# Attention's products in plain float32 on row halves and quarters of TensorE, without split operands

## The chip, the cores and the metric

The kernel runs on one core of a Trainium2 chip. The metric is the device time of one execution in microseconds (us), the median of several runs. Engines: PE is TensorE's products, PEld its weight loads, DVE is VectorE, ACT is ScalarE, POOL is GpSimd, SP is SyncE, which issues most transfers.

## The reference

Attention with a mix over the 12 heads before and after the softmax, then two MLPs, all in float32. B, H, S, D are 4, 12, 448, 64; 1792 tokens, model width 768, hidden width 2048.

```python
scores = scale * np.matmul(q, k.transpose(0, 1, 3, 2))
scores = np.einsum('bhij,hg->bgij', scores, w_pre)
scores = scores - np.max(scores, axis=-1, keepdims=True)
attn = np.exp(scores)
attn = attn / (np.sum(attn, axis=-1, keepdims=True) + 1e-09)
attn = np.einsum('bhij,hg->bgij', attn, w_post)
attn_out = np.matmul(attn, v)
...
h = x @ w_in;  r = np.maximum(h, 0.0);  x = (s * (r * r) + b) @ w_out
...
h = x @ w_in;  out = (h * np.cos(h)) @ w_out
```

## The kernel before

The rows of queries of a batch are cut into 4 blocks of 110 or 120 rows (BLOCKS); 16 blocks in all. For a block, the scores of each head (rows on partitions, 448 keys along) are copied from PSUM to SBUF and moved by DMA into a tile m with 120 partitions, 10 query rows times 12 heads, so that a product with a block-diagonal 120x120 matrix mixes the heads of 10 rows at once. Such a group of 10 rows is a tile of the loop; there are 180. m has two places, one block each.

Values that need more than one pass of fp32r are split into a high and a low part. Names and lines of the profile:
- queries (tq L389, qh and ql L394, L396) and keys (tk L320 for the first batch, L350 for the others; ks L327 to L363) are transposed by TensorE and split; queries are loaded twice and transposed once a block.
- scores (sps L420): two fp32r products a head, copies s on ACT or DVE (L431, L433), a transfer into m on SP's queue.
- The first mix: mh (L500 on ACT, L502 on POOL) is the high part of m, POOL subtracts it in place (L505), then three fp32r products (p L510 to L512).
- maximum (st L521, DVE), exp with its sum (e L528, ACT), small steps (L535, L537), and the weights w of the second mix, w_post by the reciprocals (L541, DVE).
- The second mix: plain float32, e as the stationary operand, four products of 120 columns a tile (a L550), copied to at (L562 ACT, L564 DVE).
- products with the values (vps L587): plain float32, two outputs of 64 partitions each beside one another, which is a column half of the array; copies xo (L599, L601) and transfers to x in DRAM.
- mlp (L620 on) then runs both MLPs from fp32r parts; its weights are prepared on ACT, DVE and POOL while it runs.

The order on every engine is written ahead by a planner (Plan): each step has a position, engines with costs, the steps that it follows, and holds on rings of buffers ("ps", "pa", "pp" are PSUM banks for scores and transposes, second mix, first mix: 4, 2 and 2). The planner runs through time and lets an engine take the waiting step with the lowest position whose buffers are free. The chip then executes each engine's instructions in that order. Positions come from STEP and LEAD and from offsets (OFF, W1 to W3, PRO, VW, AVP, AVL).

Of the kernel before, what the change touches and what calls it, by code (L numbers as in the profile page):

```python
# [20 lines left out]
R = 10  # L21
# [163 lines left out]
def constants():  # L185
    c = np.zeros((128, 128 + R), np.float32)
    c[:, :128] = np.eye(128)
    for r in range(R):
        c[r * 12:(r + 1) * 12, 128 + r] = 1.0
    return c  # L190


STEP = 2364.9
LEAD = 17549.5


def attention(pl, tc, q, k, v, w_pre, w_post, cst, x, mid, left, right, psl, psr):
# [4 lines left out]
    L = R * H  # L202
# [3 lines left out]
    st_p = pool(left, "a_st", 4)  # L206
# [3 lines left out]
    h_p = pool(left, "a_h", 2)  # L210
# [3 lines left out]
    q_p = pool(right, "a_q", 2, side="right")  # L214
    rk_p = pool(right, "a_rk", 2, side="right")
    rq_p = pool(right, "a_rq", 2, side="right")
# [4 lines left out]
    for name, cap in (("at", 2), ("e", N_E), ("h", 2), ("xo", 2), ("w2", 2), ("st", 4), ("m", 2), ("q", 2), ("rk", 2), ("rq", 2),   # L221
                      ("s", N_S), ("ps", 4), ("pa", 2), ("pp", 2), ("v0", 1), ("v1", 1), ("v2", 1), ("v3", 1)) + tuple((f"k{g}", 1) for g in range(6)):
# [7 lines left out]

    tiles, first = [], []
    parts = lambda n: ((0, 40), (40, 80)) if n == 0 else ((0, BLOCKS[n % 4][1]),)
    part_of = lambda n, t: sum(t * R >= r0 for r0, _ in parts(n)) - 1
    for n in range(NBLK):
        b, (i0, rows) = n // 4, BLOCKS[n % 4]
        first.append(len(tiles))
        tiles += [dict(n=n, b=b, t=t) for t in range(rows // R)]
# [21 lines left out]
    mask = one.tile([L, R], F32, name="mask")  # L259
    w12 = one.tile([L, 2, H], F32, name="w12")  # L260
    wp_h = one.tile([L, L], F32R, name="wp_h")
    wp_l = one.tile([L, L], F32R, name="wp_l")
    wq = one.tile([L, H, R], F32, name="wq")
    d_id = dma(-5200, lambda: ident, lambda: cst[:, 0:128], 65536, cost=450.0)
    d_mk = dma(CST, lambda: mask, lambda: cst[0:L, 128:128 + R], 4800)
    d_w = [dma(CST, lambda i=i: w12[:, i], lambda w=w: w.rearrange("(o h) g -> o h g", o=1).to_broadcast([R, H, H]), 5760, cost=950.0) for i, w in enumerate((w_pre, w_post))]
    hw = pl.hold("e")
    wide = lambda a: a.rearrange("p (r o) -> p r o", o=1).to_broadcast([L, R, H])

    def blk():  # L270
        hw.tile = e_p.tile([L, S], F32, tag="e", name="wblk")
        nc.vector.tensor_tensor(out=hw.tile[:, :L].rearrange("p (r h) -> p r h", h=H), in0=w12[:, 0:1].to_broadcast([L, R, H]), in1=wide(mask), op=ALU.mult)
    c0 = pl.add(LEAD - 11000, "dve", 200, blk, d_w + [d_mk], take=[hw])
    c1 = pl.add(LEAD - 11000, "act", 200, lambda: nc.scalar.activation(out=wp_h, in_=hw.tile[:, :L], func=AF.Copy, scale=D ** -0.5), [c0])
    c2 = pl.add(LEAD - 11000, "dve", 200, lambda: nc.vector.scalar_tensor_tensor(out=wp_l, in0=hw.tile[:, :L], scalar=D ** -0.5, in1=wp_h.bitcast(F32), op0=ALU.mult, op1=ALU.subtract), [c1], use=[hw])
    c3 = pl.add(LEAD - 11000, "dve", 200, lambda: nc.vector.tensor_tensor(
        out=wq, in0=w12[:, 1].rearrange("p (g o) -> p g o", o=1).to_broadcast([L, H, R]),
        in1=mask.rearrange("p (o r) -> p o r", o=1).to_broadcast([L, H, R]), op=ALU.mult), d_w + [d_mk])

    kh, k_done = {}, {}

    KW = 8 * D
    mh, m_first, m_done, m_sub, later, s_last = {}, {}, {}, {}, [], []
    m_all = m_p.tile([128, 2, 12 * S], F32R, name="m")

# [3 lines left out]
    piece = lambda z, i, n: at_all[:, z].rearrange("p c h w -> p (c h w)")[:, i:i + n]  # L291

    def first_keys(g, p):

        hk = kh[0, g] = pl.hold(f"k{g}")
        hr = scratch[0]
        raw = lambda: piece(0, 3 * g * KW, KW)[:CH].rearrange("p (x d) -> p x d", d=D)
        both = lambda: piece(0, (3 * g + 1) * KW, 2 * KW)[:CH].rearrange("p (x a d) -> p x a d", a=2, d=D)
        d = []
        for h in range(2):  # L300
            d.append(dma(p - 6000, lambda h=h: raw()[:, 4 * h:4 * h + 4].rearrange("p z d -> p (z d)"), lambda h=h: k[0, 2 * g + h].rearrange("(p z) d -> p (z d)", z=4),
                         CH * KW * 2, behind=d[-1:] + [s_open], two=g < 2, cost=500.0, rate=300.0))

        def hi(e):
            o = both()[:, :, 0].bitcast(F32R)
            if e == "pool":
                nc.gpsimd.tensor_scalar(out=o, in0=raw(), scalar1=1.0, scalar2=0.0, op0=ALU.mult, op1=ALU.add)
            else:
                nc.scalar.activation(out=o, in_=raw(), func=AF.Copy)
# [3 lines left out]
        for h in range(2):  # L313
# [3 lines left out]
            def trans(h=h, hp=hp, bank=bank, tag=tag):  # L317
                hp.tile = bank.tile([128, 512], F32, tag=tag, name="tk")[:, :S]
                for z in range(4):
                    nc.tensor.transpose(hp.tile[:, z * CH:(z + 1) * CH], both()[:, 4 * h + z].rearrange("p a d -> p (a d)"), ident[:CH, :CH])  # L320
# [88 lines left out]
    def scores(n, g, p):  # L409
        b, (i0, rows) = n // 4, BLOCKS[n % 4]  # L410
        if g == 0:
            mh[n] = pl.hold("m")
# [600 lines left out]
```

## Time and profile before

| | |
|---|---|
| time, 3 runs | median 1431.83 us (1430.13 to 1432.35) |
| profiled execution | span 1425.0 us from the first to the last instruction; its own time isn't listed, the median of the runs is 6.8 us above the span |
| TensorE products / weight loads | 1396.4 us (98%) / 1217.1 us (85%) |
| VectorE, ScalarE, POOL | 1189.2 (83%), 751.4 (53%), 635.4 us (45%) |
| transfers | 128.85 MB, mean 90 GB/s |

Busy times are sums of records and overlap where an engine works on several instructions; the mean duration of a TensorE record is longer than its share of the array's time, which shows in the chain of waits and in the distance between starts. A plain float32 product has two records, each with its weight load; an fp32r product and a transpose have one. "fp32r" products appear as f32 in the rows.

### The profile page before, as it was taken

The page shows a single profiled execution, that of the slowest core. Times are in us where ns is not written, and L with a number is a line of the kernel's source. Part 1 is how long each engine was busy: PE and PEld are TensorE (multiplying, and loading weights), DVE is VectorE, ACT ScalarE, POOL GpSimd, SP SyncE. Part 2 cuts the span into 40 slices and gives each one's busy share as a digit, 9 for nine tenths or more (in the row PEclk, how much of TensorE's full clock was granted, in tenths as well). Part 3 has the DMA queues.
Part 4 walks back from the last instruction along what each step waited for, and adds up shares of the span by engine and source line. Part 5 has one row for each costly group of instructions (what it writes and reads, how often), then busy time and mean ns, then how long its engine had stood idle before and what let it go on. Part 6 is the DMA issues. An engine that isn't in the chain of part 4 may idle for free.

```text
span 1425.0 us, 23242 instructions
## 1 busy us (share of the span) xinstructions
PE 1396.4 (98%) x8268; PEld 1217.1 (85%) x8269; DVE 1189.2 (83%) x2195; ACT 751.4 (53%) x1587; POOL 635.4 (45%) x579
## 2 busy tenths in 40 slices
PE   8999999999999899999999999999999999999999
PEld 6788888888887678888888888889999999999998
DVE  6888788688787888988887877888799999999975
ACT  4668677677677565332333232356645545455442
POOL 3746455564465354333333242334554454544431
PEclk9999999999999999999999999999999999999999
DMA  5755656565464432221211211111111121211103
GB/s 160 185 143 147 152 134 159 129 153 144 119 154 140 127 125 70 72 59 56 68 56 56 67 45 45 56 34 56 56 56 45 56 59 53 67 45 56 56 34 122
DMA packets 154233, 128.85 MB, mean 90 GB/s; under 512 B 87142, under 2 KB 141958, under 8 KB 154118
## 3 DMA queue, kind: packets, MB, share of 16 engines
q1 hardware_dynamic: 153562, 126.71, 32.3%
q8 instruction: 66, 1.08, 0.3%
q10 hardware_dynamic: 556, 0.66, 0.1%
q14 instruction: 49, 0.40, 0.1%
HBM read 77.62 MB, written 11.01 MB: 62 GB/s over the span
## 4 chain that ended last, share of the span: by engine, by line
PE 89%; DVE 5%; DMA 3%; ACT 1%; issue 1%; POOL 1%; SPq 0%; DVEq 0%; ACTq 0%
PE h L838 32%; PE o L931 16%; PE o L901 16%; PE a L550 9%; PE vps L587 5%; PE sps L420 4%; PE p L510 2%; PE p L512 2%; PE p L511 2%; DMA m<-s 1%; DVE w L541 1%; PE tq L389 1%; DVE at L564 1%; DVE st L521 1%; POOL m L505 1%
## 5 line engine op out<-in xcount | busy, mean ns | idle before, releaser
L786 POOL TENSOR_TENSOR cm<-ca,wh 128x384 f32<-128x384 f32 x128 | 160.9, 1259 | 361.3 <-ACT wh L780 353.4
L505 POOL TENSOR_TENSOR m<-m,mh 120x448 fp32r<-120x448 f32 x180 | 206.7, 1154 | 151.2 <-ACT mh L500 135.5
L838 PE MATMUL h<-m,wh 128*128 128x512 f32 x672 | 215.7, 390 | 0.0
L838 PE MATMUL h<-x,wh 128*128 128x512 f32 (+1 forms) x768 | 190.1, 338 | 1.6 <-DVE x L814 1.6
L550 PEld LDWEIGHTS a<-w,e 120*112 120x112 f32 x1440 | 166.2, 176 | 26.5 <-issue 7.7
L550 PE MATMUL a<-w,e 120*112 120x120 f32 x1440 | 173.8, 267 | 11.9 <-DVE w L541 11.5
L788 POOL TENSOR_TENSOR wl<-cm,ce 128x384 fp32r<-128x384 f32 x128 | 146.4, 1145 | 86.2 <-DVE ce L784 81.0
L838 PE MATMUL h<-m,wl 128*128 128x512 f32 x384 | 150.2, 391 | 0.0
L838 PEld LDWEIGHTS h<-x,wh 128*128 128x128 f32 x768 | 131.7, 188 | 18.2 <-DVE x L814 2.4
L838 PEld LDWEIGHTS h<-m,wh 128*128 128x128 f32 x672 | 125.2, 188 | 25.6 <-issue 0.7
L901 PE MATMUL o<-gl,wh 128*128 128x512 f32 (+1 forms) x384 | 139.6, 364 | 0.0
L901 PE MATMUL o<-gh,wl 128*128 128x512 f32 (+1 forms) x384 | 139.6, 363 | 0.0
L901 PE MATMUL o<-gh,wh 128*128 128x512 f32 (+1 forms) x384 | 139.3, 363 | 0.0
L528 ACT ACTIVATE e<-p,st 120x448 f32<-120x448 f32 x180 | 113.6, 632 | 35.9 <-DVE st L521 30.6
L878 POOL TENSOR_TENSOR tb<-ta,tb 128x512 f32<-128x512 f32 (+1 forms) x64 | 79.0, 1234 | 114.8 <-ACT tb L876 109.9
L838 PE MATMUL h<-x,wl 128*128 128x512 f32 (+1 forms) x384 | 129.8, 338 | 0.0
L521 DVE TENSOR_REDUCE st<-p 120x1 f32<-120x448 f32 x180 | 109.9, 617 | 17.7 <-PE p L512 16.5
L931 PE MATMUL o<-wh,gl 128*128 128x384 f32 x448 | 114.3, 335 | 0.0
L931 PE MATMUL o<-wh,gh 128*128 128x384 f32 x448 | 114.2, 335 | 0.0
L931 PE MATMUL o<-wl,gh 128*128 128x384 f32 x448 | 114.1, 334 | 0.0
L940 DVE TENSOR_TENSOR acc<-acc,o 128x384 f32<-128x384 f32 x196 | 99.7, 545 | 15.2 <-PE o L931 15.1
L908 DVE TENSOR_TENSOR acc<-acc,o 128x512 f32<-128x512 f32 (+1 forms) x168 | 101.5, 615 | 10.3 <-PE o L901 9.4
(102 smaller groups left out, 3161.2 us busy)
## 6 DMA issues: line engine op xcount, KB each, us to landing
m<-s SPq DMA_DIRECT2D x144, 192.5 KB
raw<-in_moe_w_in_dram SPq DMA_DIRECT2D x64, 384.0 KB
raw<-in_moe_w_out_dram SPq DMA_DIRECT2D x64, 384.0 KB
qn<-in_q_dram SPq DMA_DIRECT2D x72, 110.0 KB
m<-s SPq DMA_DIRECT2D x36, 210.0 KB
v<-in_v_dram SPq DMA_DIRECT2D x16, 336.0 KB
out_dram<-acc SPq DMA_DIRECT2D x13, 384.0 KB
rk<-in_k_dram SPq DMA_DIRECT2D x36, 112.0 KB
```

The lines of the kernel that those rows point to most:

```text
L505: a2 = pl.add(p - OFF[1] * STEP, "pool", 1110, lambda hh=hh, src=src: nc.gpsimd.tensor_tensor(out=src(), in0=src().bitcast(F32), in1=hh.ti ...
L521: nc.vector.tensor_reduce(out=hst.tile[:, 0, z:z + 1], in_=hp.tile, axis=AX, op=ALU.max, negate=True)
L528: nc.scalar.activation(out=he.tile, in_=hp.tile, func=AF.Exp, bias=hst.tile[:, 0, z:z + 1], accum_out=hst.tile[:, 1, z:z + 1])
L550: nc.tensor.matmul(out=ha.tile[:, c * L:(c + 1) * L], lhsT=he.tile[:, c * CH:(c + 1) * CH], rhs=hw2.tile[:, z], start=True, stop=True)
L786: a = pl.add(p0 + 6 * dp, "pool", 1050, lambda hm=hm, ha=ha, flat=flat: nc.gpsimd.tensor_tensor(out=hm.tile, in0=ha.tile.bitcast(F32), in1 ...
L788: got.append(pl.add(p0 + 7 * dp, "pool", 1050, lambda hm=hm, he=he, flat=flat: nc.gpsimd.tensor_tensor(out=flat(1), in0=hm.tile, in1=he.ti ...
L838: nc.tensor.matmul(out=hp.tile, lhsT=w, rhs=cols(z_, j, k)[:, 0], start=(k == 0 and y == 0), stop=(k == KD - 1 and y == 2))
L878: a = pl.add(p + 7 * dp, "pool", n * 2.4 + 100, lambda h1=h1, h2=h2: nc.gpsimd.tensor_tensor(out=h2.tile, in0=h1.tile, in1=h2.tile, op=ALU ...
L901: nc.tensor.matmul(out=hp.tile, lhsT=w, rhs=x, start=(c == 0 and y == 0), stop=(c == 1 and y == 2))
L908: a = pl.add(p, "dve", n * 1.05 + 66, lambda hp=hp, view=view: nc.vector.tensor_tensor(out=view(), in0=view(), in1=hp.tile, op=ALU.add), [ ...
L931: nc.tensor.matmul(out=hp[e].tile, lhsT=x, rhs=w[:, e * HD:(e + 1) * HD], start=(c == 0 and y == 0), stop=(c == 1 and y == 2))
L940: got.append(pl.add(p, "dve", 470, lambda e=e, hp=hp, view=view: nc.vector.tensor_tensor(out=view(), in0=view(), in1=hp[e].tile, op=ALU.ad ...
```

## The change

Attention is rewritten; mlp is as it was.
- Nothing is split. Queries, keys, m and its mixing matrix stay plain float32; POOL's subtractions, the copies mh, qh, ql and the split keys are gone.
- Keys and queries of a batch are each loaded and transposed once, two heads together (heads: tk, tq L306).
- Scores: two heads at once, each on 64 rows of the array (sps L336), two PSUM banks.
- m has 124 partitions: 4 of zeros (written once by POOL), then 120, so that 64 and 60 rows can go to two row halves. The first mix handles two tiles at once with four products, one on each quarter of the array (p L393), into two banks. Maximum and exp (L403, L409) then work on 128 partitions of 5 query rows by 12 heads of either tile.
- The second mix: for each of two tiles, 4 parts of the keys and 2 groups of 5 rows one product of 60 columns, 16 a pair, alternating between row halves (a L427). Its weights come from POOL (w L417).
- Values are loaded in three parts by heads with longer pieces (L464 reads them).
- PSUM banks: 2, 2 and 4 for "ps", "pa" and "pp". Scores take both "ps" banks, the second mix both "pa" banks. STEP is 2374.9 instead of 2364.9, LEAD 17000 instead of 17549.5, and the offsets are others.

```diff
-STEP = 2364.9
-LEAD = 17549.5
+STEP = 2374.9
+LEAD = 17000.0
...
-    ps_s = pool(psl, "a_ps_s", 4, space=PSUM)
-    ps_a = pool(psl, "a_ps_a", 2, space=PSUM)
-    ps_p = pool(psr, "a_ps_p", 2, space=PSUM, side="right")
+    ps_s = pool(psl, "a_ps_s", N_PS, space=PSUM)
+    ps_a = pool(psl, "a_ps_a", N_PA, space=PSUM)
+    ps_p = pool(psr, "a_ps_p", N_PP, space=PSUM, side="right")
...
+    def heads(what, b, g, p):
...
+        d = dma(p - 6000, lambda: raw(True), lambda: src[b, 2 * g:2 * g + 2].rearrange("h (p z) d -> p z h d", z=4), CH * 8 * D * 4,
+                [s_open] if b == 0 else [], take=[hr] if b else [], behind=m_done[0][-1:] if b else [], two=b == 0 and g < 2, rate=300.0)
...
-                for y in range(2):
-                    nc.tensor.matmul(out=hp.tile, lhsT=hq.tile[y][:, h % 4], rhs=hk.tile[:, z], start=(y == 0), stop=(y == 1))
-            a = pl.add(p + QZ * z, "pe", 410.0, prod, k_done[b, g] + [q_done[n, g // 2]] + m_first.get(n, []), take=[hp] + ([] if h else [hm]), use=[hk, hq])
+        def prod():
+            for z in range(2):
+                hp[z].tile = ps_s.tile([128, 512], F32, tag="s", name="sps")[:rows, :S]
+                nc.tensor.matmul(out=hp[z].tile, lhsT=hq.tile[64 * z:64 * z + 64, i0:i0 + rows], rhs=hk.tile[64 * z:64 * z + 64], start=True, stop=True, tile_position=(64 * z, 0))
+        a = pl.add(p, "pe", 790.0, prod, [t_done["k", b, g], t_done["q", b, g]], take=hp, use=[hk, hq], behind=last_s[-1:])
...
-            nc.tensor.matmul(out=hp.tile, lhsT=wp_h, rhs=hh.tile, start=True, stop=False)
-            nc.tensor.matmul(out=hp.tile, lhsT=wp_l, rhs=hh.tile, start=False, stop=False)
-            nc.tensor.matmul(out=hp.tile, lhsT=wp_h, rhs=src(), start=False, stop=True)
-        a = last_mix[n % 2] = pl.add(p - OFF[2] * STEP, "pe", 615, mix, [a2, c1, c2], take=[hp], use=[hh, mh[n]])
+            for z in range(2):
+                src = mh[pair[z]["n"]].tile.bitcast(F32)[:, pair[z]["t"]]
+                for y in range(2):
+                    nc.tensor.matmul(out=hp[y].tile[64 * z:64 * z + 64], lhsT=wp[64 * y:64 * y + (K if y else 64)], rhs=src[64 * y:64 * y + (K if y else 64)], start=True, stop=True, tile_position=(64 * y, 64 * z))
+        a = pl.add(p - OFF[0] * STEP, "pe", 840, mix, [d for n in ms for d in m_done[n]] + [c1, m_zero], take=hp, use=[mh[n] for n in ms])
...
-            nc.vector.tensor_tensor(out=hw2.tile[:, :m], in0=wq.rearrange("p (o g) r -> p o (g r)", o=1).to_broadcast([L, m, L]),
+            nc.gpsimd.tensor_tensor(out=hw2.tile, in0=wq.rearrange("p (o g) r -> p o (g r)", o=1).to_broadcast([128, 2, K]),
...
-                for c in range(4):
-                    nc.tensor.matmul(out=ha.tile[:, c * L:(c + 1) * L], lhsT=he.tile[:, c * CH:(c + 1) * CH], rhs=hw2.tile[:, z], start=True, stop=True)
-            a = pl.add(p_, "pe", 820, mixt, [aw], take=[ha], use=[he, hw2])
+            for c in range(4):
+                for y in range(2):
+                    for z in range(2):
+                        nc.tensor.matmul(out=ha[z].tile.rearrange("p (c g r) -> p c g r", c=4, g=H)[:, c, :, y * G:(y + 1) * G], lhsT=he.tile[64 * z:64 * z + K, y, c * CH:(c + 1) * CH],
+                                         rhs=hw2.tile[64 * z:64 * z + K, y], start=True, stop=True, tile_position=(64 * z, 0))
+        a = pl.add(p, "pe", MIXT, mixt, [aw], take=ha, use=[he, hw2])
...
+MIXT = 1100.0
...
+N_PS, N_PA, N_PP = 2, 2, 4
```

How the order of TensorE's instructions moves, in two places. In the steady part before (p is the first mix, sps scores, a the second mix, tq transposed queries; xN is a count of instructions in a row, with a plain float32 product counted once):

```order
L512 MATMUL p<-m,wp_h 120x448
L420 MATMUL sps<-ks,qh 110x448
L420 MATMUL sps<-ks,ql 110x448
L550 MATMUL a<-w_873,e 112x120 x4
L420 MATMUL sps<-ks,qh 110x448
L420 MATMUL sps<-ks,ql 110x448
L510 MATMUL p<-mh,wp_h 120x448
L511 MATMUL p<-mh,wp_l 120x448
L512 MATMUL p<-m,wp_h 120x448
```

and in the steady part of the change:

```order
L336 MATMUL sps<-kt,qt 110x448 x2
L393 MATMUL p<-m,wp 64x448 x4
L427 MATMUL a<-w_628,e 112x12x5 x16
L336 MATMUL sps<-kt,qt 110x448 x2
L393 MATMUL p<-m,wp 64x448 x4
L336 MATMUL sps<-kt,qt 110x448 x2
L427 MATMUL a<-w_685,e 112x12x5 x16
```

The three products of a tile's first mix become four for two tiles on quarters, and stand between scores and second mixes, which are on row halves. Over the whole of attention, 79 groups of first mixes now stand between groups of another form of the array.

At the start before (tk transposed keys, of two heads in 8; block 0 has 120 rows):

```order
L389 MATMUL tq<-ident,at 128x120 x4
L420 MATMUL sps<-ks,qh 120x448
L420 MATMUL sps<-ks,ql 120x448
L320 MATMUL tk<-ident,at 128x112 x8
L420 MATMUL sps<-ks,qh 120x448
L420 MATMUL sps<-ks,ql 120x448
```

and in the change (110 rows is block 1):

```order
L306 MATMUL tk<-ident,at 128x112 x4
L306 MATMUL tq<-ident,at 128x112 x4
L336 MATMUL sps<-kt,qt 120x448 x10
L336 MATMUL sps<-kt,qt 110x448 x6
L393 MATMUL p<-m,wp 64x448 x8
L336 MATMUL sps<-kt,qt 110x448 x2
L393 MATMUL p<-m,wp 64x448 x8
L427 MATMUL a<-w_351,e 112x12x5 x16
```

Before, each group of keys is followed by its scores, and the first mixes begin when a third of block 0 is in m. Now nearly all keys and queries of the first batch are transposed ahead of block 0's scores, and the first mix waits for the whole of block 0, with part of block 1's scores ahead of it.

## Rows read from the trace of the kernel before

**Rows 1.** The page's engine shares and TensorE's granted clock in 40 slices.
```profile
PE 1396.4 (98%) x8268; PEld 1217.1 (85%) x8269; DVE 1189.2 (83%) x2195; ACT 751.4 (53%) x1587; POOL 635.4 (45%) x579
...
PEclk9999999999999999999999999999999999999999
```

**Rows 2.** Three stretches: us, busy time and instructions of each engine, clock, DMA share, GB/s.
```profile
0.00:46.00 46.00, 38.99 (x230) 28.25 (x231) 31.74 (x61) 23.03 (x51) 21.22 (x30) 1.00 0.60 167
46.00:240.00 194.00, 187.49 (x1405) 161.93 (x1405) 158.04 (x326) 137.85 (x329) 102.98 (x103) 1.00 0.61 150
240.00:440.00 200.00, 196.64 (x1479) 171.60 (x1478) 157.92 (x330) 146.47 (x351) 112.03 (x113) 1.00 0.55 140
```

**Rows 3.** Chain of waits, 54 to 70 us: start us, us, what.
```profile
54.07 0.20 PE p L510
...
55.74 0.41 PE sps L420 x2
56.15 0.82 PE a L550 x8
...
58.82 0.38 PE tq L389 x4
```

**Rows 4.** TensorE's groups up to 510 us: count, busy us, mean ns, idle before.
```profile
L550 PE MATMUL a<-w,e 120*112 120x120 f32 x1440 | 173.8, 267 | 11.9 <-DVE w L541 11.5
...
L420 PE MATMUL sps<-ks,qh 128*110 128x448 f32 (+1 forms) x192 | 78.5, 409 | 0.0
...
L389 PE MATMUL tq<-ident,qn 110*128 110x110 f32 (+1 forms) x180 | 24.6, 260 | 0.5 <-ACT s L431 0.5
...
L350 PE MATMUL tk<-ident,rk 112*128 112x112 f32 x72 | 9.9, 259 | 0.0
...
L320 PE MATMUL tk<-ident,at 112*128 112x112 f32 x48 | 5.7, 261 | 1.6 <-DVE at L311 1.6
...
L389 PE MATMUL tq<-ident,at 120*128 120x120 f32 x12 | 1.7, 265 | 0.0
```

**Rows 5.** Chain of waits, 440.5 to 445 us.
```profile
440.50 0.82 PE a L550 x8
441.32 3.26 PE vps L587 x32
444.57 0.39 PE p L510
```

**Rows 6.** TensorE's weight loads: two in order of time, then groups by line.
```profile
444.50 0.18 PEld L510 LDWEIGHTS p<-mh,wp_h 120*120 120x120 f32 x1 [0.34 <-ACT mh L500]
444.61 0.18 PEld L511 LDWEIGHTS p<-mh,wp_l 120*120 120x120 f32 x1
...
L550 PEld LDWEIGHTS a<-w,e 120*112 120x112 f32 x1440 | 166.2, 176 | 26.5 <-issue 7.7 <-PE p L512 5.8 <-ACT m L813 3.0
L587 PEld LDWEIGHTS vps<-at,v 112*64 112x64 f32 x682 | 47.0, 136 | 18.8 <-ACT at L562 1.2 <-issue 0.9 <-PE a L550 0.6
```

**Rows 7.** Other engines' groups up to 480 us.
```profile
L505 POOL TENSOR_TENSOR m<-m,mh 120x448 fp32r<-120x448 f32 x180 | 206.7, 1154 | 151.2 <-ACT mh L500 135.5 <-DMA rk<-in_k_dram 10.5
...
L564 DVE COPY at<-a 112x480 f32<-112x480 f32 x105 | 68.6, 654 | 17.4 <-PE a L550 16.2
...
L431 ACT ACTIVATE s<-sps 110x448 f32<-110x448 f32 (+1 forms) x126 | 67.6, 542 | 28.2 <-PE sps L420 13.3 <-DMA m<-s 8.0 <-issue 5.5
...
L500 ACT ACTIVATE mh<-m 120x448 fp32r<-120x448 f32 x109 | 62.7, 576 | 44.5 <-PE p L511 25.9 <-DMA m<-s 8.4 <-PE a L550 3.8
...
L541 DVE TENSOR_TENSOR w<-wq,st 120x240 f32<-120x240 f32 x90 | 56.2, 625 | 1.9
```

**Rows 8.** TensorE in order of time at the first mixes; releaser in brackets.
```profile
24.52 0.36 PE L510 MATMUL p<-mh,wp_h 120*120 120x448 f32 x1
...
33.93 1.86 PE L550 MATMUL a<-w,e 120*112 120x120 f32 x16 [1.47 <-DVE w L541]
...
42.52 1.86 PE L550 MATMUL a<-w,e 120*112 120x120 f32 x16 [0.61 <-DVE w L541]
```

More of the change, by code (lines that the diff above doesn't have):

```diff
@@ L229, in dma, with copy @@
         return pl.add(pos, "sp", cost, lambda: nc.sync.dma_start(out=out(), in_=in_()), after, take, use, nbytes=nbytes, behind=behind, rate=rate)
+    def copy(e, out, in_):
+        if e == "act":
+            nc.scalar.activation(out=out, in_=in_, func=AF.Copy)
+        else:
+            nc.vector.tensor_copy(out=out, in_=in_)
     tiles, first = [], []
-    parts = lambda n: ((0, 40), (40, 80)) if n == 0 else ((0, BLOCKS[n % 4][1]),)
-    part_of = lambda n, t: sum(t * R >= r0 for r0, _ in parts(n)) - 1
     for n in range(NBLK):
-        b, (i0, rows) = n // 4, BLOCKS[n % 4]
         first.append(len(tiles))
-        tiles += [dict(n=n, b=b, t=t) for t in range(rows // R)]
+        tiles += [dict(n=n, b=n // 4, t=t) for t in range(BLOCKS[n % 4][1] // R)]
     NTL = len(tiles)
@@ L332, in keys @@
-    def keys(b, g, p):
-        hk = kh[b, g] = pl.hold(f"k{g}")
-        hr = pl.hold("rk")
-        raw = lambda: hr.tile
-        def load(h):
-            if h == 0:
-                hr.tile = rk_p.tile([CH, 4, 2 * D], F32, tag="rk", name="rk")
-            return raw()[:, :, h * D:(h + 1) * D]
-        d = []
-        for h in range(2):
-            d.append(dma(p - 6000, lambda h=h: load(h), lambda h=h: k[b, 2 * g + h].rearrange("(p z) d -> p z d", z=4), CH * KW * 2,
-                         take=[] if h else [hr], behind=d if h else m_done[0][-1:]))
-        hp = pl.hold("ps")
+    turned, t_done = {}, {}
@@ L452, in attention @@
[L452 to L460 removed]
+            m_done[n] = []
+        hm, hk, hq = mh[n], turned["k", b, g], turned["q", b, g]
+        hp, hs = [pl.hold("ps"), pl.hold("ps")], pl.hold("s")
+        def prod():
+            for z in range(2):
+                hp[z].tile = ps_s.tile([128, 512], F32, tag="s", name="sps")[:rows, :S]
+                nc.tensor.matmul(out=hp[z].tile, lhsT=hq.tile[64 * z:64 * z + 64, i0:i0 + rows], rhs=hk.tile[64 * z:64 * z + 64], start=True, stop=True, tile_position=(64 * z, 0))
@@ new lines, in place @@
+        def place(z):
+            if hm.tile is None:
+                hm.tile = m_all[:, n % 2].rearrange("p (t j) -> p t j", j=S)
+            return hm.tile.bitcast(F32)[4:4 + 2 * K].rearrange("(r h) t j -> r h t j", h=H)[:, 2 * g + z, :T]
+        for z in range(2):
+            m_done[n].append(dma(p + 1300, lambda z=z: place(z), lambda z=z: hs.tile[:rows, z], rows * S * 4, ev[z:z + 1], take=[hm] if g == 0 and z == 0 else [], use=[hs],
+                                 behind=m_done[n][:1], cost=870.0, two=n == 0))
@@ L461, in attention @@
+    for g in range(NG):
+        for what in "kq":
+            heads(what, 0, g, PRO[0] * g)
+        scores(0, g, PRO[0] * g + PRO[1])
     for n in range(1, NBLK):
@@ L466, in attention @@
             lo, hi = pos(first[n - 1]) + W2[0] * STEP, pos(first[n]) - W2[1] * STEP
-        w = (hi - lo) / 6
-        ps = [lo + w * (g + .5) for g in range(6)]
+        w = (hi - lo) / NG
+        ps = [lo + w * (g + .5) for g in range(NG)]
         if kk == 0:
-            for g in range(6):
-                keys(b, g, pos(first[n - 2]) + (W3[0] + g * W3[1]) * STEP)
-        for g in range(6):
-            if g % 2 == 0:
-                queries(n, g // 2, ps[g] - w - 2500)
+            for g in range(NG):
+                for what in "kq":
+                    heads(what, b, g, ps[g] - W3[0] * STEP)
+        for g in range(NG):
             scores(n, g, ps[g])
```

356 lines of the change are left out of this document (115 added, 241 removed).

## Prediction, made before the change was run

> **What bounds the kernel now.** I read the page's shares first: TensorE is busy 98% of the span with its clock at the upper level (2.4 GHz) throughout [rows 1]. The table of stretches then shows where this holds: from 46 to 440 us TensorE has 187.5 of 194 and 196.6 of 200 us, while VectorE stands at 158, ScalarE at 138 to 146 and POOL at 103 to 112 us [rows 2]. That stretch is the attention that the change rewrites; what comes after about 500 us is the two MLPs, which it doesn't touch. The chain of waits in the middle of attention [rows 3] is TensorE instruction after TensorE instruction. So the price of a product there is the time its columns hold the array, and what I compare is TensorE's time before and after. The profiled execution has a span of 1425.0 us; its own time isn't listed. The median of the runs is 6.8 us longer, and I put that difference on top of every sum.
>
> **What one product costs.** One fp32r product of 448 columns takes 0.20 us, two take 0.41: one pass over the columns [rows 3]. A plain float32 product shows twice in the records (1440 records for 720 products, [rows 4]); eight of them, 120 columns each, take 0.82 us, so 0.1025 us a record, 246 clocks for 120 columns: two passes a record, four a product [rows 3, 4]. Scaled by columns, a plain product of 448 columns takes 4 times 448 columns, 2 x 0.1025 x 448/120 = 0.765 us. It is dearer than three fp32r products (0.61) unless several run at once. That they can is shown for halves of the columns: the 32 records of one product with the values (16 products, 230 columns, two outputs of 64 partitions) take 3.26 us [rows 5], where 32 x 460 columns in a row would be 6.13.
>
> **The sum, in a pair of tiles** (90 pairs: 1440 records of the second mix are 180 tiles of 8 [rows 4]).
> - First mix. Before: 6 fp32r products, 6 x 0.205 = 1.23 us [rows 3]. Now four plain ones on four quarters: 0.765 if all four run at once. 90 x 0.465 = 41.8 us less. No row shows quarters or row halves; the bounds are 0.765 (all at once) and 4 x 0.765 = 3.06 (one by one). The nearest row, the column halves, has full overlap, so I take 0.765.
> - Scores. Before 192 x 0.41 = 78.7 us; now 96 pairs of heads on two row halves, 96 x 0.765 = 73.4: 5.3 less (bounds: 0.765 and 1.53 a pair).
> - Second mix. Before 2 x 0.82 = 1.64 us. Now 16 products of 60 columns, 8 on each row half, 16 records a half. A record streams 51 ns, but it needs a weight load of 112 columns first. After a stop, one load follows the other by 0.11 us at 120 columns [rows 6], and loads of 64 and 112 columns last 136 and 176 ns [rows 6], 0.83 ns a column more; so 112 columns hold the path for about 95 ns. Before, that hid behind 102 ns of streaming; now the load is the longer. 16 x 95 = 1.52 us a pair, 10.8 us less in all. Bounds: 16 x 51 = 0.82 (loads cost nothing) and 32 x 95 = 3.04 (the halves' loads take turns). I take 1.52, because it is the loads' own rate.
> - Transposes. 312 before (180 + 12 of queries, 72 + 48 of keys, [rows 4]), 192 now, as queries are turned once a batch instead of once a block, and without the doubled operand; 0.38 us for four [rows 3]: 11.4 us less. Products with the values: the same 24 groups.
> - Changing between forms of the array. After the a-products end (440.50 + 0.82) the 32 records take 3.26 us, where 16 x 460 columns are 3.07, and the next product takes 0.39 instead of 0.20 [rows 5]: about 0.19 us going in and 0.19 coming out. In the order of instructions a group of another form (full array, row halves, quarters, column halves) follows 45 times before and 210 times now; 165 x 0.19 = 31 us more. Bounds: nothing (if row halves and quarters change freely) and twice that.
>
> Together -41.8 - 5.3 - 10.8 - 11.4 + 31 = -38 us. The rows price only changes to and from column halves; counting those alone (42 now) the sum would be -69. The Trainium skill, TensorEngine Tiling (Array Packing), Key Properties, says that any change of tiling mode drains the engine, without a price; by that rule all 210 changes count, and the sum is -38.
>
> **What else moves.** POOL loses 180 subtractions of 1154 ns, ScalarE 109 copies of 576 ns (POOL the other 71), VectorE 90 weightings of 625 ns [rows 7]; 90 weightings half as wide come to POOL. None of it was what TensorE waited for longest (11.5 us for the weightings, [rows 4]), so I cost it at nothing. The cover is TensorE's own work: exp, sum, reciprocal and weighting of a pair lie behind the other products, since four banks hold two pairs. A weighting of 120 elements on POOL lies between 0 and the 1.15 us of 448 elements. Should the cover fail, each pair shows a piece of the chain maximum, two exps, small steps, weighting. VectorE and ScalarE also lose the split of queries and keys and gain 48 copies of 0.54 to 0.65 us [rows 7], so neither becomes the bound. SP issues the same 192 transfers into m; 93 loads of parts of queries (110 or 120 KB) and 48 of keys (112 KB) become 48 of 224 KB by the code, some 5 MB less, so the queue isn't later in the steady part.
>
> At the start it is: keys and queries of the whole first batch (12 x 224 KB) are loaded and issued ahead of the first transfer into m, then all of block 0 (12 x 210 KB: 120 rows of 448 floats) must land, 5.3 MB; at the 167 GB/s of the first 46 us [rows 2] that is 32 us. Before, the first mix ran at 24.52, but the second mixes came in pieces up to 42.52, and TensorE waited [rows 8]. Now the first second mix would come near 38 us, after which nothing need stop. I put 3 us on top (from -5 to +12); the order around this place stands above.
>
> **Forecast:** -38 + 3 = -35 us: a span of 1390, 1397 as a run.
>
> **Rivals.**
> - *Second mix cheaper than its loads.* Two halves may load faster than the full array's rate suggests. At 0.82 a pair, 90 x 0.70 = 63 us more go: 1334; half way 1365. For: short loads start within the shadow of running products. Against: the spacing of [rows 6].
> - *The gain is waited away.* Scores now take both of two PSUM banks and need two copies before the next pair, where four single banks turned before; the second mix likewise takes both of its two. Copies take 0.54 to 0.65 us [rows 7]; if 0.37 us of each of the 96 score groups lay open, 35 us would come back: 1432, no change. Against: between two score groups stands at least a mix or a second mix in the order, 0.765 us or more.
> - *Slower: load and product of one half take turns.* In the second mix each record would be 95 + 51 = 146 ns, a pair 2.34 us; 90 x 0.82 = 74 us more than my sum: 1471. It decides from a pair of 1.52 + 35/90 = 1.91 us on. Against it: before, a record takes 102 ns in all with a load of about 95 ahead of it [rows 3, 6], so there a load runs under its predecessor on the same rows. The Trainium skill, TensorE: Matmul & The Clock Gate, Part 3, says a load overlaps running products only where the row groups differ; it would give this rival. This trace differs, as the 102 ns say.
> - *The change doesn't do what it says: quarters run two at a time.* First mix 1.53 a pair, 90 x 0.765 = 69 us more: 1466. It decides from 1.15 us a mix on. For: only two at once is shown anywhere.
>
> **How the numbers follow.** Forecast 43% (its own range 1375 to 1422, from the start, from the price of a change of form and from some stalls), cheaper second mix 26%, waited away 13%, turns 9%, quarters in twos 7%, the rest 2%. Predicted is 1397. The low end, 1340, takes in most of the cheaper second mix; the high end, 1445, the waits and somewhat more; the two slower rivals lie beyond, 16%. About 0.2% is what a measurement can tell from no change. Faster: nearly all of the first two and a third of the third, 73%; within 0.2%: 5%, from the waits; slower: 22%.
>
> **What would show it.** In the changed profile: the MLP lines as before; TensorE's work in attention some 35 us shorter and still with few waits. A mix group of about 0.77 us plus a change; scores 0.77 a pair; a second mix near 1.5 us with loads one after the other at 95 ns in each half (0.8 would show rival one, 2.3 the turns, a mix of 1.5 the twos). Gaps of 0.1 to 0.2 us at changes of form. TensorE idle behind copies of s or a would show the waits. I'd be wrong in kind if VectorE, ScalarE or the transfers into m ended most of TensorE's waits, or if time moved in the MLPs.

## The result, and the profile of the changed kernel

The changed kernel takes 1410.12 us (median of 4 runs, 1409.28 to 1412.58), the kernel before 1431.35 us on the same chip (4 runs, 1430.13 to 1432.35). The ratio is 0.9855, 95% interval 0.9838 to 0.9873: 21 us faster. Forecast were 35 us and 1397; the sign is right, the time lies inside the range, and the gain is about three fifths of the forecast. The profiled run of the changed kernel took 1410.2 us with a span of 1408.4, 16.6 us less than the span of before.

The page's shares and granted clock, to be held against [rows 1]:

```profile
PE 1383.4 (98%) x9753; PEld 1103.6 (78%) x9753; DVE 1095.8 (78%) x2052; ACT 665.8 (47%) x1385; POOL 429.7 (31%) x415
...
PEclk6899999999999999999999999999999999999999
```

TensorE is still the bound, but its clock is no longer at the upper level throughout: the first two of the 40 slices (35 us each) stand at 0.6 and 0.8. The stretches (us, busy time and instructions of each engine, clock, DMA share, GB/s) answer to [rows 2]:

```profile
0.00:46.00 46.00, 35.69 (x105) 14.27 (x109) 14.28 (x24) 7.68 (x12) 9.26 (x5) 0.61 0.69 151
46.00:240.00 194.00, 192.37 (x2214) 120.35 (x2208) 127.98 (x283) 113.62 (x270) 16.12 (x42) 1.00 0.53 145
240.00:440.00 200.00, 198.31 (x2379) 127.55 (x2376) 133.89 (x302) 116.92 (x285) 19.36 (x46) 1.00 0.48 143
440.00:460.00 20.00, 17.21 (x190) 13.76 (x191) 15.20 (x34) 13.27 (x31) 4.95 (x7) 0.83 0.31 99
```

From 46 to 440 us TensorE is busy 390.7 of 394 us at the full clock; VectorE, ScalarE and POOL all have less to do than in [rows 2]. Two stretches are out of line: the first 46 us, and the end of attention from 440 us on (clock 0.83 in the fourth row). The middle is read from the chain of waits at 300 us (start us, us, what), as [rows 3] were:

```profile
302.82 0.80 PE sps L336 x4
303.61 0.91 PE p L393 x8
304.52 1.71 PE a L427 x32
306.24 0.80 PE sps L336 x4
```

The same chain at 56 us has the groups in another order:

```profile
56.39 0.94 PE sps L336 x4
57.33 1.53 PE a L427 x32
58.86 0.91 PE p L393 x8
```

A first mix (p), a second mix (a) and a pair of scores (sps) take 0.91 + 1.71 + 0.80 = 3.42 us, and the chain is TensorE behind TensorE. The prediction's terms for these three were 0.765 + 1.52 + 0.765 and, since scores and second mix are both on row halves, two changes of form of 0.19: 3.43. By the second excerpt the change shows on the group that follows it: a pair of scores takes 0.94 behind a first mix and 0.80 behind a second mix, a second mix 1.71 behind a first mix and 1.53 behind scores, so 0.14 to 0.18 a change. The bare groups are a little dearer than the terms (0.80 for 0.765, 1.53 for 1.52), the changes a little cheaper than 0.19.

The start, TensorE in order of time, answers to [rows 8]:

```profile
16.01 3.29 PE L336 MATMUL sps<-kt,qt 64*120 64x448 f32 x4
...
20.96 1.85 PE L336 MATMUL sps<-kt,qt 64*120 64x448 f32 x2
23.52 1.85 PE L336 MATMUL sps<-kt,qt 64*120 64x448 f32 x4 [0.72 <-DVE s L235]
...
36.56 1.83 PE L336 MATMUL sps<-kt,qt 64*110 64x448 f32 x4 [0.76 <-DVE s L235]
39.97 1.83 PE L336 MATMUL sps<-kt,qt 64*110 64x448 f32 x4 [1.58 <-DVE s L235]
...
44.24 3.27 PE L393 MATMUL p<-m,wp 64*64 64x448 f32 x16
...
51.13 1.78 PE L427 MATMUL a<-w,e 60*112 60x60 f32 x32
```

The first pair of scores runs at 16.01 us; in the kernel before the first scores ran at 9.24. From 21 to 44 us a pair then comes every 2.5 to 2.7 us: 1.85 of product (0.80 to 0.95 at the full clock), then 0.6 to 0.8 in which TensorE waits for a copy. Once it waits 1.58 us (39.97), as the copy itself waits until an earlier transfer into m has freed its buffer. Two stretches of it show the clock at 0.50, its lower level of 1.2 GHz, and the queues at 86 and 162 GB/s:

```profile
20.00:25.00 5.00, 4.28 (x12) 1.59 (x10) 1.25 (x2) 0.96 (x1) 0.00 (x0) 0.50 0.30 86
...
30.00:35.00 5.00, 3.49 (x10) 0.95 (x8) 1.25 (x2) 1.09 (x2) 0.00 (x0) 0.50 0.49 162
```

The first mix comes at 44.24 us (24.52 before), the first second mix at 51.13 (30.60 before).

One more thing differs at the start that the section on the change doesn't name. The kernel before puts bfloat16 products of zeros (idle) into TensorE's order there, and its clock stands at 1.00; the changed kernel keeps only those of the first 5 us. The groups of the first 46 us, before and changed:

```profile
L253 PE MATMUL idle<-rest 128*128 128x512 bf16 x24 | 7.9, 474 | 1.2 <-DVE rest L245 1.2
...
L256 PE MATMUL idle<-rest 128*128 128x512 bf16 x9 | 4.0, 631 | 1.2 <-DVE w L268 1.2
```

Where the time went is seen when both traces are read at the same share of the second mix's records (start of that record, us; worked out from the single records):

```
share of the second mix done   before   changed   difference
first record                     30.6      51.1      +20.5
 5%                              53.1      63.8      +10.7
 7%                              60.5      72.5      +12.0
50%                             258.0     259.0       +1.0
97%                             470.4     447.9      -22.5
last record                     478.3     458.8      -19.5
last product with the values    491.2     473.9      -17.3
first output product of MLP 1   514.5     498.0      -16.5
```

In between the two kernels do their other work in another order, so single lines swing (50%), but the ends are plain: 10.7 to 12.0 us behind at the start, 34.5 us won from 7% to 97%, 6 us lost again up to the first output product; after that the MLPs keep the 16.5 us.

TensorE's busy time between the records at 7% and 97% says where the 34.5 us come from (before, then changed):

```profile
60.50:470.40 409.90, 398.89 (x3011) 343.64 (x3010) 327.13 (x676) 293.60 (x701) 222.68 (x222) 1.00 0.55 142
...
72.50:447.90 375.40, 371.51 (x4384) 238.46 (x4380) 249.27 (x554) 219.64 (x525) 35.51 (x85) 1.00 0.50 143
```

TensorE works 27.4 us less and waits 7.1 us less (3.9 instead of 11.0). Summed by group from the single records, changes of form included, the first mixes take 28 us less (105 to 77), the second mixes the same (137), the scores 3 more (67 to 70), the transposes 4 less (22 to 18), the products with the values the same.

### The profile page after: what moved, and what is told of

It reads as the page before. It is cut to its first block, busy times and chain, and to the rows that moved or that the text cites. A ratio compares the mean times of both kernels' runs of the same rounds, so it can differ in the third digit from the quotient of the medians.

```text
span 1408.4 us, 25444 instructions
## 1 busy us (share of the span) xinstructions
PE 1383.4 (98%) x9753; PEld 1103.6 (78%) x9753; DVE 1095.8 (78%) x2052; ACT 665.8 (47%) x1385; POOL 429.7 (31%) x415
## 4 chain that ended last, share of the span: by engine, by line
PE 96%; DVE 1%; DMA 1%; ACT 1%; SPq 0%; issue 0%; POOL 0%; DVEq 0%; POOLq 0%
PE h L704 33%; PE o L797 17%; PE o L767 16%; PE a L427 11%; PE sps L336 7%; PE p L393 6%; PE vps L464 5%; PE tq L306 1%; PE tk L306 1%; DMA m<-s 0%; SPq L229 0%; DMA at<-in_q_dram 0%; DMA m<-x 0%; DVE s L235 0%; DVE x L680 0%
## 5 line engine op out<-in xcount | busy, mean ns | idle before, releaser
L427 PEld LDWEIGHTS a<-w,e 60*112 60x112 f32 x2880 | 153.6, 176 | 50.8 <-issue 29.3
L427 PE MATMUL a<-w,e 60*112 60x60 f32 x2880 | 161.6, 261 | 3.7 <-POOL w L417 3.5
L417 POOL TENSOR_TENSOR w<-wq,st 128x120 f32<-128x120 f32 x90 | 35.5, 396 | 396.5 <-DVE st L413 306.9
L409 ACT ACTIVATE e<-p,st 128x448 f32<-128x448 f32 x180 | 113.2, 630 | 55.4 <-DVE st L403 41.6
L403 DVE TENSOR_REDUCE st<-p 128x1 f32<-128x448 f32 x180 | 109.5, 618 | 21.7 <-PE p L393 19.4
L336 PE MATMUL sps<-kt,qt 64*110 64x448 f32 (+1 forms) x384 | 109.3, 613 | 6.7 <-DVE s L235 5.3
```

The lines of the kernel that those rows point to most:

```text
L336: nc.tensor.matmul(out=hp[z].tile, lhsT=hq.tile[64 * z:64 * z + 64, i0:i0 + rows], rhs=hk.tile[64 * z:64 * z + 64], start=True, stop=True, ...
L403: nc.vector.tensor_reduce(out=hst.tile[:, 0, y:y + 1], in_=hp[y].tile, axis=AX, op=ALU.max, negate=True)
L409: nc.scalar.activation(out=he.tile[:, y], in_=hp[y].tile, func=AF.Exp, bias=hst.tile[:, 0, y:y + 1], accum_out=hst.tile[:, 1, y:y + 1])
L427: nc.tensor.matmul(out=ha[z].tile.rearrange("p (c g r) -> p c g r", c=4, g=H)[:, c, :, y * G:(y + 1) * G], lhsT=he.tile[64 * z:64 * z + K, ...
```

## Experiments

Each ratio is to the kernel before as it ran beside the experiment; its median was 1428.3 to 1431.4 us over the series, so kernels of different series are compared by their ratios.

**Is the second mix bound by its weight loads?** e2_half loads and writes 56 of a chunk's 112 keys and leaves the others out of the second mix and of the products with the values; the streamed columns stay.

```
- lhsT=he.tile[64 * z:64 * z + K, y, c * CH:(c + 1) * CH]
+ lhsT=he.tile[64 * z:64 * z + K, y, c * CH:c * CH + CH // 2]
```

> The changed kernel with half of the second mix's stationary columns: each product loads 56 columns of e instead of 112 and so computes half of the keys; the copies and the products with the values then work on 56 partitions. It leaves out half of the sum over the keys. Streamed columns, records and the order stay the same. Theory: the second mix is bound by its weight loads, 95 ns a record in each half of the rows, against 51 ns of streaming. Then a record falls to 50 to 55 ns, a group of 32 records from 1.53 to 1.72 us to 0.85 to 1.0, and 90 groups give 55 to 65 us: 1345 to 1360, if nothing else becomes the bound. Rival: the records are bound by something that columns do not change, such as their issue: the group stays above 1.5 us and the time at 1407 to 1413.

Measured: 1362.45 us, ratio 0.9545 (0.9524 to 0.9565), 2 us above the expected range. Chain of waits at 63 and 309 us:

```profile
63.47 0.91 PE p L393 x8
64.38 0.83 PE a L427 x32
65.21 0.94 PE sps L336 x4
...
309.00 0.98 PE a L427 x32
309.98 0.95 PE sps L336 x4
```

With half the stationary columns and the same streaming a second mix without a change of form falls from 1.53 to 0.83 us: the loads of 112 columns set its time. The edit moves the changes of form too. A second mix with 56 columns pays nothing behind a first mix (0.83) and 0.15 behind scores (0.98), and scores behind it pay (0.94, where 0.80 stood): next to the others it behaves as a product on quarters. The Trainium skill, TensorE: Matmul & The Clock Gate, LDWEIGHTS (loading the stationary operand), gives columns divided by 1.2 in ns, an estimate of 93 ns for 112 columns and 47 for 56. Here 1.53/16 = 96 ns agrees with the first; 0.83/16 = 52 ns is about the 51 ns of streaming, so the second is not tested.

**Can the loads be shortened without leaving work out?** e4_quarters puts scores and second mix on quarters: 64 stationary columns at most, four loads side by side. Keys are taken 64 at a time, in 7 parts and one that repeats the last.

```
+ for w in range(2):
+     j = 64 * min(2 * c + w, 6)
+     nc.tensor.matmul(out=ha[z].tile[64 * w:64 * w + 64]..., lhsT=he.tile[64 * z:64 * z + K, y, j:j + 64],
+                      rhs=hw2.tile[64 * z:64 * z + K, y], start=True, stop=True, tile_position=(64 * z, 64 * w))
```

> The changed kernel with scores and second mix on quarters too, in the form that the first mix has: scores of 64 rows and the remaining 46 or 56 rows beside one another; the second mix in parts of 64 keys (seven, with the last one computed twice so that both halves of the columns are filled), keys in their own order, values loaded to match. Theory: a weight load of 64 columns takes 55 ns, so a second mix takes about 0.9 us plus 0 to 0.1, where it took 1.53 to 1.72, and scores, first and second mix no longer change the form between them: a pair of score products falls from 0.84 to 0.95 us to about 0.8, a first mix from 0.91 to about 0.8. Sum: 90 x 0.7 + 96 x 0.1 + 79 x 0.1 = 80 us less TensorE work; with the other engines then at 80 to 90% I expect a part of it to be waited away: 1340 to 1370. Rival: 64 records of products in 0.9 us are more than TensorE can issue, or quarters change nothing: the second mix stays at 1.5 us or more and the time above 1395.

Measured: 1363.99 us, ratio 0.9544 (0.9522 to 0.9565). Chain at 310 us:

```profile
310.57 0.97 PE a L437 x64
311.54 0.76 PE p L401 x8
312.30 0.75 PE sps L344 x8
```

The three together take 2.48 us instead of 3.42, and no change of form is left among them: 0.76 and 0.75 are the bare 0.765 of the columns. That would be 85 us on 90 pairs; by the ratios 44 came. 28 us of the difference are waits: TensorE now waits 31 of the 394 us from 46 to 440 (3 in the changed kernel), 6.3 us of it for POOL's weightings, the rest in smaller pieces for copies, exps and transfers that had cover until then. The other 13 are not accounted for.

**Load or change of form in the scores?** A pair of scores takes 0.80 to 0.95 us where the columns need 0.765. e5_squart puts the scores alone on quarters, so that loads shrink from 110 columns to 64, but the number of changes of form in TensorE's order stays (219 in the changed kernel, 223 in e5_squart; 84 in e4_quarters, 46 before).

```
+ for y in range(2):
+     c0, c1 = ((0, 64), (64, rows))[y]
+     nc.tensor.matmul(out=hp[z].tile[c0:c1], lhsT=hq.tile[64 * z:64 * z + 64, i0 + c0:i0 + c1], ..., tile_position=(64 * z, 64 * y))
```

> The changed kernel with the scores alone on four quarters (64 and 46 or 56 query columns of each head, each on its own quarter) and the second mix still on row halves. Theory (a pair of scores takes 0.84 to 0.96 us where its columns need 0.75, because the load of 110 stationary columns stands open, and a first mix pays 0.16 us more when it does not follow a group of the same form): scores fall to 0.75 to 0.78 us a pair and a first mix beside them to 0.75 to 0.80; 96 x 0.13 = 12 us from the scores, up to 10 more from the mixes that follow scores: 1388 to 1400 us where the changed kernel took 1410. Rival (loads and changes of form cost nothing, the columns alone set the time): 1407 to 1413.

Measured: 1409.26 us, ratio 0.986 (0.9841 to 0.9878), no gain. Chain at 106 us:

```profile
105.91 1.72 PE a L430 x32
107.62 0.90 PE sps L339 x6
108.52 1.72 PE a L430 x32
...
270.88 0.91 PE p L396 x8
271.80 0.75 PE sps L339 x8
```

My theory was wrong in its cause: behind second mixes a pair still takes 0.90 us, now that the change of form stands there; behind a first mix, with no change, it takes 0.75. And a second mix behind scores now takes 1.72, where it took 1.53. It is the change that costs, about 0.15 to 0.19 us; at most 0.05 (0.80 to 0.75) is left for the load. The time lies in the rival's range, but its reason falls too: changes are not free, their number merely stayed. The Trainium skill, TensorEngine Tiling (Array Packing), Key Properties, says that a change of tiling mode drains the engine. These rows agree in that the group behind a change takes longer; they don't show what happens in between.

**What paces the start?** First the clock alone: e1_warm adds bfloat16 products of zeros behind the transposes and scores of the start.

```
+ if b == 0: warm(p + 1, 3, a)
...
+ if n == 0 or n == 1 and g < 3: warm(p + 1 if n == 0 else 16000.0 + g, 4 if n == 0 else 8, a)
```

> The changed kernel with products of zeros on TensorE between the transposes and scores of the start (bf16, 128x512, three after each transposition, four or eight after each pair of score products up to the first mix); the rest is the same. Theory: the start costs what it does because TensorE falls to its lower clock there (granted 0.5 from 10 to 45 us), so that a pair of scores takes 1.9 us instead of 0.9. Then the clock stays at the upper level, the scores of block 0 come 1.7 instead of 2.4 to 2.6 us apart, the first mix comes some 6 to 9 us before 44.2 us, and the time is 5 to 9 us below the changed kernel's 1410, so 1401 to 1405. Rival: the start is set by the loads and by the transfers into m, whatever the clock: first mix within 2 us of 44.2, time 1408 to 1412.

Measured: 1422.2 us, ratio 0.996 (0.9942 to 0.9977), outside the ranges of theory and rival. TensorE at the start:

```profile
31.66 1.01 PE L347 MATMUL sps<-kt,qt 64*120 64x448 f32 x2
33.38 1.01 PE L347 MATMUL sps<-kt,qt 64*120 64x448 f32 x2 [0.72 <-DVE s L235]
34.33 1.04 PE L266 MATMUL idle<-rest 128*128 128x512 bf16 x4
35.29 1.01 PE L347 MATMUL sps<-kt,qt 64*120 64x448 f32 x2
...
54.29 1.73 PE L406 MATMUL p<-m,wp 64*64 64x448 f32 x16
```

The clock was at 1.00 from 25 us on, yet the first mix came 10 us later. 8 of the 10 are lost ahead of the first scores, which run at 24.19 us (16.01 in the changed kernel), to the added products and to 4.03 us in which TensorE waits for VectorE. Then a pair comes every 3.63 us (31.66, 35.29), where it came every 2.5 to 2.7: its two products (two records each) no longer run side by side but one after the other, 1.01 us each, with 0.72 of waiting for a copy between them, and the added products cost another 0.97 us in an engine that works in order. So the run doesn't price the clock alone. What it leaves is the theory that the turn of two PSUM banks paces the start: a pair holds both, and the next needs a copy. e6_banks lets block 0's scores take the four banks of the first mix, empty until then, and puts each pair behind its own transposes; e7_qbanks does the same on e4_quarters.

```
- hp, hs = [pl.hold("ps"), pl.hold("ps")], pl.hold("s")
+ ring = "pp" if n == 0 else "ps"
+ hp, hs = [pl.hold(ring), pl.hold(ring)], pl.hold("s")
...
- PRO = (1283.6, 9149.2)
+ PRO = (1283.6, 2000)
```

> The changed kernel with block 0's scores in the four PSUM banks that belong to the first mix and stand empty until then, and each pair of scores ordered behind its own transposes. Theory (the start is paced by the turn score pair, copy, next score pair, since a pair holds both banks of its ring; the low clock only lengthens the score part of that turn): score pairs of block 0 stand back to back, the first mix comes at 34 to 39 us instead of 44.2, the first second mix at 41 to 46 instead of 51.1, and the time is 1400 to 1406 us. Rival (the transfers pace it: loads of whole keys and queries, then 12 transfers into m): first mix still at 42 to 45, time 1408 to 1412.

> The kernel with scores and second mix on quarters (1364 us), with the same change of banks and order at the start as in e6_banks. Theory of the turn of two banks: first mix at 33 to 38 us instead of 41.6, 4 to 9 us less: 1355 to 1360. Rival (transfers pace the start): 1362 to 1366.

Measured: e6_banks 1402.28 us, ratio 0.9807 (0.9788 to 0.9826); e7_qbanks 1355.24, ratio 0.9486 (0.9458 to 0.9514). e6_banks at the start:

```profile
8.50 1.02 PE L337 MATMUL sps<-kt,qt 64*120 64x448 f32 x4
...
21.54 5.35 PE L337 MATMUL sps<-kt,qt 64*120 64x448 f32 x12
...
34.52 3.27 PE L394 MATMUL p<-m,wp 64*64 64x448 f32 x16
...
41.41 1.78 PE L428 MATMUL a<-w,e 60*112 60x60 f32 x32
```

Three pairs now run back to back, the first mix comes 9.7 us earlier with the clock still at 0.50 from 20 to 25 and from 30 to 35 us, and at 5% of the second mixes the kernel is level with the one before (54.1 against 53.1 us). The ratio says 7 us won, the two spans 11.4. So the rival, that the transfers pace the start by themselves, is refuted. But the edit changes two things. The first scores run 7.5 us earlier (8.50 against 16.01), which is the order; from there to the first mix it takes 26.0 us, where it took 28.2. No run changes the banks without the order, so how much the turn of two banks costs by itself is not shown.

**What loses 6 us at the end of attention?** I suspected MLP products that stand ahead of the last products with the values. e8_tail and e9_qtail were to move those; the condition in the edit picks the half before the last, so its three products went into other banks and earlier, and the last three stayed.

```
- hp, ho = pl.hold("ps"), pl.hold("xo")
+ hp, ho = pl.hold("pp" if late else "ps"), pl.hold("xo")
...
- AVL = (4.673, 5603.6)
+ AVL = (3.0, 5.0)
```

> The kernel e6_banks with the last half's three products with the values in PSUM banks of the first mix (free by then) and ordered as early as their inputs allow, so that two of them follow the last second mix at once and 12 MLP products stand ahead of the third, as in the kernel before; in the changed kernel and in e6_banks 36 MLP products stand ahead of the last one and 18 of them (4.35 us) right between. Theory (the way of x from the last product with the values through its copy, its store, its load and its split to the first MLP sets the end, 23 to 24 us, so these 18 products lie on the path there and 2 us of waits with them): last product with the values 5 to 8 us earlier, 1394 to 1399 us where e6_banks took 1402. Rival (the MLP products have to be done anyway, ahead or behind, so nothing is gained): 1400 to 1404.

> The kernel e7_qbanks (scores and second mix on quarters, start in the first mix's banks, 1355 us) with the same change of the last products with the values. Theory: 4 to 8 us less, 1347 to 1352. Rival: 1353 to 1357.

Measured: 1416.04 us, ratio 0.9903 (0.9877 to 0.993), and 1366.16, ratio 0.9546 (0.9519 to 0.9573): both slower than the kernels they were made from, by 14 and 9 us by the ratios. The last second mixes of e8_tail:

```profile
446.73 2.15 PE L428 MATMUL a<-w,e 60*112 60x60 f32 x32 [1.17 <-ACT at L233]
451.68 3.24 PE L428 MATMUL a<-w,e 60*112 60x60 f32 x32 [2.80 <-POOL w L418]
455.68 3.27 PE L428 MATMUL a<-w,e 60*112 60x60 f32 x32 [0.75 <-ACT at L233]
```

They stand alone, without scores or MLP products between them, each waits for a copy of an earlier result (at) or for POOL's weighting (w), and the clock falls (0.50 from 450 to 460 us, and 3.24 us for a second mix). That says nothing on the question asked. e10_tail and e11_qtail move only the 24 MLP products behind the last half's products; e6_again is the yardstick.

```
+ if 4 * b + 2 * hf + 2 == NBLK: v_last.append(a)
...
- prod, w_done[nn, c, 0] + xd + [a] + ...
+ prod, w_done[nn, c, 0] + xd + [a] + (v_last if (u, c) in ((units[0], 1), (units[1], 0)) else []) + ...
```

> The kernel e6_banks with one difference in the order of TensorE: the 24 MLP products that stood ahead of the last half's products with the values (18 of them right between the first and the other two) follow them. (e8_tail, whose edit picked the half before the last by its condition, left them where they were.) Theory (x's way from the last product with the values through copy, store, load and split to the first MLP sets the end): last product with the values 4.4 to 6 us earlier, 1395 to 1398 us where e6_banks took 1402. Rival (the MLP products have to be done anyway, and TensorE's sum of work sets the end): 1400 to 1404.

> The kernel e7_qbanks with the same difference in order. Theory: 4 to 6 us less than its 1355: 1349 to 1351. Rival: 1353 to 1357.

> e6_banks once more, unchanged, beside e10_tail on the same chip: 1399 to 1405 us, the yardstick for e10_tail.

Measured: e10_tail 1401.23 us, ratio 0.9804 (0.9789 to 0.9819), beside e6_again's 1403.15, ratio 0.9816 (0.98 to 0.9832): not told apart. e11_qtail 1351.12 us, ratio 0.945 (0.9438 to 0.9463), 4 us under e7_qbanks in another series, with intervals that touch; its last product with the values starts at 421.9 us, e7_qbanks's at 422.2, so the way that the theory named did not get shorter. So these MLP products are not, or not alone, what the end of attention loses. e6_banks and e6_again are one kernel, and their stretch from 440 to 460 us differs:

```profile
440.00:460.00 20.00, 19.28 (x166) 14.84 (x168) 12.88 (x29) 7.69 (x16) 7.30 (x6) 0.91 0.23 65
```

in e6_banks, and in e6_again

```profile
440.00:460.00 20.00, 17.82 (x121) 13.60 (x120) 9.55 (x22) 7.61 (x17) 7.30 (x6) 0.66 0.13 43
```

with spans of 1397.0 and 1402.3. At 97% of the second mixes the two are 1.4 us apart (437.5 and 438.9), at the first output product 5.2 (486.6 and 491.9). So two executions of one kernel differ at this end by nearly as much as the 6 us in question, with the clock lower in the longer one. In the changed kernel TensorE waits from 440 to 500 us for (us, times, longest):

```profile
PE h L704 <- DVE x L680: 3.8, 2, 2.8
PE a L427 <- POOL w L417: 2.8, 2, 2.2
PE h L704 <- ACT x L679: 1.4, 1, 1.4
```

These 8.0 us are no more than the 8.1 that the kernel before waits in the same way from 440 to 520 us. By the table, 3 of the 6 us lie in the last 3% of the second mixes and 2 between the last of them and the last product with the values. What they are beside the lower clock, and how much of them is chance, stays open.

**What paces the start of the best kernel?** e12_best adds to e11_qtail a fourth buffer for copied scores, and makes the two weight tables behind block 0's copies.

```
+ late_w = pl.add(-400, "none", 7000, None, d_w + [d_mk])
...
- N_S = 3
+ N_S = 4
```

> The kernel e11_qtail with two more changes at the start, to see whether copies of scores that wait pace what is left of it: the two small weight tables are made on VectorE after block 0's copies instead of among them (in e6_banks VectorE stood 3.9 us behind their transfer), and four instead of three buffers between the scores' copies and their transfers into m. Theory: first mix 3 to 6 us earlier than e11_qtail's (some 34 us), 1345 to 1349 us. Rival (the loads of whole keys and queries and the 12 transfers into m pace it now): first mix within 1.5 us of e11_qtail's, 1349 to 1354.

Measured: 1351.24 us, ratio 0.9445 (0.941 to 0.948); the first mix at 32.78 us, 1.1 before e11_qtail's. Its chain there:

```profile
15.72 5.26 DMA at<-in_q_dram
...
25.96 6.13 DMA m<-s
32.78 1.73 PE p L403 x16
```

By this chain loads and transfers pace it now, as the rival had it. e11_qtail and e12_best, 79 us under the kernel before, are the fastest found.

## Why the prediction was right in sign and too large

- **First mix, 0.765 us on four quarters at once:** right. In e4_quarters it stands bare at 0.76; in the changed kernel 0.91 with its change of form. The rival "quarters in twos" (from 1.15 us on) is refuted.
- **Second mix, 16 loads of 95 ns:** right, 1.53 us where no change of form stands ahead of it, 96 ns a load. The rows gave only a range, from 93 ns (112 columns of 0.83) to 103 (0.11 us less 8 columns), so it is in part luck that the value was met so closely. "Load and product take turns" (from 1.91 us on) and "cheaper than its loads" both fall, the latter also by e2_half. The choice that decided was to take the load's own rate from [rows 6].
- **Changes of form, 0.19 us:** right: 0.14 to 0.19, and their number rose by 173 (46 to 219), where 165 were counted. 3.43 predicted and 3.42 measured for the three groups is closer than the parts. e5_squart, where the changes stay, and e4_quarters, where they go, show that it is they. That a change among row halves, quarters and the full array costs like one to column halves was an assumption, and it held.
- **"The gain is waited away":** refuted; TensorE waits 3 us from 46 to 440, where it waited 10 before. The cover held here; in e4_quarters, with shorter products, it does not.
- **Steady part, -38 us:** 34.5 us on 90% of the pairs, which is 38 on all, but the number was met by luck. The sum was of TensorE's work alone, and that fell by 27 us (30 on all): the second mixes with their changes save nothing, the scores cost 3 us more, the transposes save 4. The other 7 us are waits that went away, a term that I put at nothing. My reason doesn't hold against [rows 4]: the weightings that I listed as leaving VectorE are the very ones that TensorE waited for longest (11.5 us up to 510; in this stretch 4.7, and 1.3 for those of POOL now).
- **Start, +3 us (-5 to +12): the step that failed.** Some 11 us are lost at 5 to 7% of the second mixes, and 2 to 3 of steady gain are in that already, so it cost 13 to 14. I summed bytes: 5.3 MB by 32 us, then "nothing need stop". But the bytes were not ready to move: from 20 to 30 us the queues moved 86 to 106 GB/s. The first scores ran 6.8 us later than before (16.01 against 9.24), behind nearly all transposes, and then came in turn with their copies, a pair every 2.5 to 2.7 us. I had that order in front of me and priced its bytes alone; the turn I had named as a rival in the steady part, where other products cover it, and not here, where nothing does. e6_banks, which changes order and banks, wins about half of the loss back by its ratio. The lower clock (0.50 from 10 to 45 us), with most of the products of zeros gone, I had not foreseen at all. It makes the product in that turn 1.85 us instead of 0.9; what it costs in time is not shown, as e1_warm changed more than the clock.
- **The end of attention, at nothing:** 6 us lost between these two executions, cause open.
- **6.8 us around the span:** wrong as a reading, harmless in the sum, since it sets the 35 us off from the median of the runs. Every run whose span is listed is 1.8 us longer than it, so the profiled execution of before would have taken some 1426.8 us, less than any of its four runs here. The two medians lie 21 us apart, the two spans 16.6, and what is read from this pair of traces can be off by those 4.6 us.

Together -38, 13.5 at the start and 6 to 8 at the end make -16.5 to -18.5, beside 16.6 between the spans. That 1410 lies inside the range is owed to its width: the start alone went beyond its own bounds.

## What to carry to other kernels

Cost a packed product by the longer of two, its columns and the loads that share its rows, and add the change of form where its neighbour has another; then count the changes in the order of the instructions (some 0.15 us each here, and 219 of them). Price the waits that a change takes away as well as the work. Cost a start apart from the steady part: ask when the first product of each kind can run, and which buffers take turns when no other work lies between. And products put in to hold the clock take their own time: in e1_warm they made the start longer.

## What the runs showed of the hardware that was not expected

- Four plain float32 products of 448 columns on four quarters take 0.75 us together, the time that the columns of a single one come to (0.765).
- Loads on different quarters run side by side: 32 products (64 records) with 64 stationary columns, 16 records to a quarter, take 0.97 us, 60 ns each; loads of 112 columns on two row halves need 96.
- A change of form costs 0.14 to 0.19 us, seen on the group behind it. Products with 56 stationary columns on a row half pay none behind products on quarters and 0.15 us behind products with 110 or 120 columns on the same row halves (e2_half).
- TensorE's granted clock stood at 0.50 from 10 to 45 us of the changed kernel, with the engine busy 4.97 of 5 us (15 to 20 us, transposes and scores) as well as 3.49 of 5 (30 to 35 us, scores and waits). From 5 to 10 us, busy 3.21 of 5 us, it had stood at 0.98. It was 0.76 from 45 to 50 us, when first mixes and scores followed without a gap, and 1.00 after that.
